# One transfer per store for the last two token tiles, a last half tile in two pieces, and a new issue order

## The chip, the cores and the metric

The kernel runs on one core of a Trainium2 chip. The metric is the device time of one execution in microseconds (us). The kernel before took 256.01 us as the median of three runs (255.62 to 257.51). One further execution was profiled; it took 256.55 us. A core has five engines that run their own instruction streams and meet at semaphores: PE (matrix multiply), DVE (vector), ACT (scalar functions, also copies), POOL, and SP, which here only issues DMA transfers. All numbers called "the profile" come from that one profiled execution, with times counted from the start of its span.

## The reference

For 2048 tokens of width 640, `x` is normalised (`xn`), and three things are added: `x` itself, a gated feed-forward block on `xn`, and a long convolution branch multiplied by `xn`.

```python
def _A_ref(q, k, v, shift_k, ssm_k, ssm_D):
    k_shift = sum(k_pad[:, t:t + S, :] * shift_k[:, ks - 1 - t] for t in range(4))
    kv = k_shift * v
    y = irfft2(rfft2(kv_pad) * rfft2(kf_pad))[..., :S, :]     # causal convolution of length 2048
    y = y + kv * ssm_D
    return q * y
def _B_ref(x, w_gate, w_up, w_down):
    return (sigmoid(x @ w_gate) * (x @ w_up)) @ w_down        # 640 -> 1728 -> 640
xn = layernorm(A_q)
out = A_q + _A_ref(xn, A_k, A_v, ...) + _B_ref(xn, ...)
```

Inputs and output are bfloat16, 2048 x 640.

## The kernel before, in words

**Token tiles.** The 2048 tokens are 16 tiles of 128 rows (`NQ = 16`). The tile `acc` [128, 16, 640] holds `x` at first and collects the result. Partition 32q + n of tile m holds token row 64n + 16q + m, so the output in memory, seen from a tile, has two outer dimensions: q (4 groups) and n (32 rows in each), the view `oq4` with axes q, n, m, d.

**Feed-forward block.** Four "rows" of four tiles (tr = 0 to 3). `rec_fc` (matmuls on line 770) computes a gate group and an up group for each of 14 blocks of 128 hidden columns, five matmuls of 512 columns each. ACT applies the sigmoid, DVE multiplies, and the product is written to `hT`. `rec_down` (line 786) multiplies `hT` by the down weights `wd`: for each token tile two halves of 320 output columns, each in two parts of seven matmuls. DVE adds each half from PSUM into `acc` (line 798). All these groups share two PSUM banks, named g: a new group waits until the group two places before it was read out. Weights for the gate and up groups come through four buffers named w.

**Convolution branch.** It is a four-stage transform over 10 sub-blocks of channels (two halves of five). Stage 1 is line 508, stage 2 line 528, the products lines 548 to 567, stage 3 line 580, stage 4 line 612. For sub-blocks 3 to 9 the products need the two partition halves exchanged, which two DMAs do (line 548, `P<-S`, the swap); the exchanged copy has one buffer. Stage 4 runs once per half, in four pieces (u = 0 to 3) of 128 small matmuls each; its result is multiplied and added into `acc` by DVE (lines 620 and 621). The tiles 14 and 15 of the down projection start only when all of that has been added (`PRM["ML"] = 14`).

**Stores.** `store` (line 630) writes ranges of tiles to `out`, in four DMAs of 32 partitions each (one per q), all issued by SP. The calls at the end of the kernel are for tiles 0-7, 8-11, 12-13, 14, the first half of tile 15 and the second half of tile 15.

**What sets the order.** Every operation is recorded by `plan.op` and gets a number. Nothing is scheduled at run time: the list `ORDER` names all numbers in the order in which they are emitted, and `ON_DVE` says which of the movable copies run on DVE instead of ACT. Each engine then executes its own operations in that order, waiting at each for its inputs and buffers. The numbers that the text below speaks of are these (they name the same operation in both lists):

- 80, 92: reciprocal and normalisation of token tile 1; 82, 83: statistics of token tile 2 (all DVE). 98: transposition of normalised tile 1 on PE.
- 653 and 654: transposition for the second row on PE, and the copy of its result out of PSUM.
- 872: gate group of hidden block 1, row 3. 887: the load of up weights for hidden blocks 4 to 7 of row 3; it reuses a w buffer. 893: the up group of block 5, row 3, the first user of that load in the new order.
- 549 to 555: stage 2 of the last sub-block. 557 and 558: its swap. 559 to 566: its products (DVE). 567 and 569: its stage 3 (PE). 911: the DVE product for hidden block 8 of row 3.
- 948 to 951: down projection of tile 14; 952, 953: its two additions. From 954 on the numbers differ between the lists: tile 15.

A few lines carry most of the ordering around the end:

```python
def table(self):
    dve = set(ON_DVE)
    for i in ORDER:
        o = self.ops[i]
        o.on = next(iter(o.engs)) if len(o.engs) == 1 else "DVE" if i in dve else "ACT"
    return [self.ops[i] for i in ORDER]
```

Of the kernel before, what the change touches and what calls it, by code (L numbers as in the profile page):

```python
# [16 lines left out]
ALU = mybir.AluOpType  # L17
# [4 lines left out]
P = 128  # L22
NQ = S // P
# [19 lines left out]
def _dft_tables():  # L43
# [34 lines left out]


ORDER = [  # L80
    3, 5, 0, 8, 2, 7, 6, 42, 71, 12, 10, 13, 4, 11, 72, 14, 16, 1, 19, 73, 74, 75, 91, 76, 607, 86, 608, 18, 43, 96,
    77, 61, 97, 78, 79, 104, 62, 63, 64, 81, 20, 80, 92, 87, 17, 82, 98, 83, 643, 15, 88, 84, 85, 148, 99, 93, 89,
    645, 100, 149, 60, 625, 644, 58, 90, 94, 67, 626, 102, 101, 27, 150, 103, 613, 621, 66, 44, 615, 623, 65, 106, 68,
    154, 622, 57, 624, 614, 616, 617, 619, 105, 153, 609, 56, 59, 22, 611, 618, 108, 620, 599, 601, 610, 612, 600, 29,
    107, 109, 646, 602, 157, 32, 158, 648, 603, 605, 112, 647, 650, 113, 30, 151, 649, 651, 652, 635, 637, 111, 110,
    152, 604, 636, 31, 606, 638, 23, 155, 26, 631, 627, 633, 632, 25, 156, 24, 629, 118, 117, 634, 21, 639, 641, 120,
    628, 630, 640, 642, 667, 35, 114, 661, 116, 668, 671, 115, 662, 665, 121, 119, 36, 133, 122, 123, 127, 681, 124,
    673, 39, 37, 682, 128, 684, 674, 677, 134, 45, 129, 679, 135, 653, 680, 38, 654, 683, 663, 131, 657, 136, 658,
    664, 33, 47, 666, 125, 48, 675, 126, 137, 34, 54, 172, 655, 656, 676, 163, 678, 669, 164, 659, 162, 130, 660, 28,
    670, 165, 672, 689, 691, 167, 739, 741, 132, 166, 181, 690, 692, 168, 53, 740, 721, 182, 742, 831, 723, 743, 693,  # L90
    744, 159, 298, 160, 41, 171, 722, 745, 724, 698, 40, 161, 700, 730, 169, 49, 732, 699, 701, 702, 52, 183, 832,
    734, 731, 300, 50, 178, 51, 736, 170, 173, 733, 175, 179, 735, 180, 174, 685, 176, 737, 738, 138, 177, 195, 687,
    196, 725, 727, 299, 199, 305, 186, 185, 184, 201, 202, 197, 46, 686, 688, 187, 188, 198, 189, 200, 203, 301, 833,
    707, 709, 190, 791, 69, 192, 302, 55, 726, 712, 194, 728, 193, 708, 729, 141, 70, 710, 213, 227, 191, 714, 214,
    713, 711, 139, 303, 228, 715, 215, 95, 716, 703, 718, 229, 304, 218, 217, 233, 230, 204, 206, 231, 704, 140, 142,
    216, 219, 771, 705, 706, 220, 234, 221, 208, 694, 696, 224, 695, 232, 697, 205, 717, 226, 249, 254, 719, 753, 225,
    207, 143, 222, 746, 772, 755, 720, 250, 209, 251, 754, 210, 253, 223, 757, 756, 252, 211, 758, 767, 759, 260, 235,
    237, 239, 212, 255, 263, 760, 256, 768, 236, 238, 261, 262, 288, 264, 290, 763, 265, 266, 267, 269, 770, 270, 241,
    242, 257, 240, 243, 244, 258, 834, 268, 836, 747, 285, 407, 748, 146, 289, 306, 751, 245, 271, 273, 412, 275, 291,
    286, 786, 247, 788, 749, 259, 287, 761, 318, 272, 294, 145, 762, 246, 750, 319, 297, 248, 752, 320, 321, 764, 324,  # L100
    325, 410, 274, 322, 276, 279, 409, 765, 280, 292, 787, 323, 277, 278, 766, 315, 789, 769, 835, 293, 326, 838, 308,
    309, 837, 327, 295, 296, 317, 281, 307, 839, 840, 310, 777, 282, 790, 779, 811, 283, 316, 778, 312, 782, 284, 328,
    329, 340, 354, 330, 331, 784, 783, 780, 334, 785, 341, 144, 773, 332, 342, 812, 360, 358, 355, 333, 413, 356, 774,
    311, 792, 781, 359, 345, 775, 361, 776, 357, 336, 813, 313, 335, 822, 338, 362, 815, 824, 408, 337, 823, 314, 339,
    363, 825, 376, 793, 795, 344, 351, 353, 343, 346, 794, 411, 147, 796, 817, 404, 347, 352, 427, 814, 819, 365, 364,
    366, 826, 428, 406, 429, 431, 367, 418, 816, 370, 405, 433, 371, 432, 828, 867, 368, 414, 383, 818, 374, 434, 369,
    797, 820, 821, 375, 799, 372, 373, 827, 348, 349, 829, 350, 798, 830, 384, 385, 430, 417, 435, 800, 387, 416, 419,
    415, 806, 436, 866, 424, 801, 386, 425, 808, 802, 377, 426, 421, 378, 379, 380, 388, 389, 803, 449, 390, 804, 463,
    450, 420, 805, 464, 422, 807, 437, 453, 860, 809, 451, 381, 841, 810, 465, 467, 468, 423, 382, 469, 470, 439, 854,
    397, 861, 864, 438, 391, 392, 855, 440, 858, 872, 394, 452, 441, 466, 455, 874, 848, 456, 460, 454, 849, 852, 393,  # L110
    462, 443, 856, 442, 398, 399, 857, 461, 400, 444, 445, 859, 401, 471, 844, 457, 447, 458, 459, 472, 446, 448, 490,
    473, 842, 485, 486, 499, 500, 845, 847, 474, 843, 846, 487, 501, 503, 504, 476, 475, 477, 479, 505, 478, 850, 506,
    489, 862, 496, 502, 498, 480, 863, 851, 481, 865, 482, 507, 873, 508, 483, 886, 887, 488, 853, 491, 493, 877, 497,
    492, 494, 527, 875, 878, 876, 510, 512, 515, 484, 529, 528, 531, 533, 879, 880, 516, 509, 532, 881, 534, 511, 513,
    514, 883, 868, 519, 530, 870, 395, 882, 520, 926, 884, 535, 536, 571, 869, 521, 523, 927, 871, 901, 495, 903, 885,
    892, 537, 396, 928, 402, 522, 585, 894, 902, 906, 524, 904, 526, 592, 539, 578, 893, 525, 538, 517, 888, 549, 541,
    895, 896, 518, 905, 550, 890, 897, 551, 907, 555, 553, 899, 540, 898, 543, 544, 542, 900, 929, 556, 545, 554, 552,
    931, 930, 557, 558, 889, 932, 908, 403, 891, 559, 910, 547, 909, 911, 921, 561, 563, 912, 923, 922, 560, 914, 924,
    548, 913, 917, 546, 915, 564, 567, 562, 565, 566, 569, 933, 568, 570, 579, 580, 916, 925, 934, 919, 581, 582, 918,
    935, 583, 920, 572, 936, 584, 573, 574, 937, 940, 575, 586, 576, 577, 962, 587, 938, 589, 588, 590, 960, 942, 939,  # L120
    591, 967, 966, 593, 594, 941, 595, 963, 596, 944, 597, 598, 943, 945, 946, 947, 968, 948, 950, 971, 969, 949, 964,
    961, 952, 951, 965, 953, 975, 970, 972, 974, 973, 954, 955, 958, 979, 976, 956, 978, 977, 9, 957, 959, 980, 982,
    981, 983
]
ON_DVE = [
    101, 103, 133, 34, 140, 144, 820, 568, 582, 574, 589, 588, 595
]


# [90 lines left out]
def kernel(  # L220
# [82 lines left out]
    def pe(dur, n, fn, **kw):  # L303
        plan.op({"PE": (dur * 1e-3, fn)}, ni=2 * n, **kw)
# [320 lines left out]

    def store(m0, m1, pri, d0=0, d1=DM):
        key = [("acc", m, x) for m in range(m0, m1) for x in range(4)] if d1 - d0 == DM else (
            [("fin", m, d0 // 320) for m in range(m0, m1)] + [("cv", m // 4) for m in range(m0, m1)])
        for q in range(4):
            dma(lambda e, q=q: e.dma_start(oq4[q][:, m0:m1, d0:d1], acc[32 * q:32 * q + 32, m0:m1, d0:d1]), 32,  # L630
                2 * (d1 - d0) * (m1 - m0), r=key, w=[("out", m0, d0, q)], pri=pri)
# [145 lines left out]
    def rec_down(tr, out):  # L777
        for t4 in range(4):
            m = 4 * tr + t4
            pd = [f"pd{m}_{i}" for i in range(2)]  # L780
            parts = [(0, 7, (0,)), (7, 14, (0,)), (0, 7, (1,)), (7, 14, (1,))]
            for c0, c1, ii in parts:
                def f(c0=c0, c1=c1, t4=t4, pd=pd, ii=ii):
                    for fc in range(c0, c1):
                        for i in ii:
                            nc.tensor.matmul(tl[pd[i]][:, 0:320], lhsT=hT[:, fc, t4 * P:(t4 + 1) * P],  # L786
                                             rhs=wd[:, fc, 320 * i:320 * i + 320],
                                             start=(fc == 0), stop=(fc == NFC - 1))
                kw = dict(r=[("hT", fc) for fc in range(c0, c1)] + [("wd", fc) for fc in range(c0, c1)] +
                          ([("z",)] if c1 == 14 else []) + ([("cv", u) for u in range(4)] if m >= PRM["ML"] and c0 == 0 else []) + ([("last",)] if m == NQ - 1 and c0 == 0 else []),  # L790
                          w=[(pd[i],) for i in ii] + ([("last",)] if m == NQ - 2 and c1 == 14 else []), pri=gt())
                if c0 == 0:
                    kw["alloc"] = [(pd[i], "g") for i in ii]
                n = len(ii) * (c1 - c0)
                pe(n * MD, len(ii) * (c1 - c0), f, **kw)
                pos[0] += n * MD * 1e-3
            for i in range(2):
                dve(320, 1, lambda i=i, m=m, pd=pd: nc.vector.tensor_tensor(  # L798
                    acc[:, m, 320 * i:320 * i + 320], tl[pd[i]][:, 0:320], acc[:, m, 320 * i:320 * i + 320], ALU.add),
                    r=[(pd[i],)], w=[("fin", m, i)], c=[("acc", m, q) for q in range(4)], pri=gt() - 2000)  # L800


# [90 lines left out]
    store(12, 14, 244.0)  # L893
    store(14, 15, 246.0)
    store(15, 16, 247.0, d1=320)
    store(15, 16, 248.0, d0=320)
    plan.emit(plan.table(), make)


# [28 lines left out]
```

## Time and profile before

| What | Value |
|---|---|
| Median of three runs | 256.01 us |
| Profiled execution, its own time | 256.55 us |
| Its span (first to last instruction) | 254.8 us (254.75) |
| PE busy / share of span | 241.0 us / 95% |
| DVE busy | 199.8 us / 78% |
| ACT busy | 179.0 us / 70% |
| Granted PE clock, mean | 0.998 |
| Stores to out: number, us from issue to landing | 24; 1.4 shortest, 2.3 median, 3.7 longest |

The profiled execution took 1.8 us more than its span; that part lies outside the recorded instructions. It is 0.54 us slower than the median of the three runs, so a difference worked out in the span is applied to the median. Rows of the profile name a line of the kernel, an engine, and the operation with the names of what it writes and reads. A bracket behind a row of the timeline says how long the engine had been idle before it and what ended that. "SPq" is SP's queue of issued DMAs; the time of such a row is the issuing, not the transfer. PE's busy time is an upper bound: matmuls overlap, so a row of 0.30 us can follow another after 0.136 us.

### The profile page before, as it was taken

The numbers are of one execution on the slowest core, as the hardware profiler recorded it, in microseconds if no ns is written. First come the engines' busy times: TensorE is split into PE (matmuls) and PEld (weight loads), VectorE is DVE, ScalarE is ACT, GpSimd is POOL, SyncE is SP. The second block draws the span as 40 slices with busy tenths as digits, with TensorE's granted clock in tenths as the row PEclk, the third lists the DMA queues.
The fourth block names the chain that finished last, engine by engine and source line by source line (L and its number), as shares of the span: only waits on it lengthen the run. The fifth ranks groups of instructions, "written<-read, shape, count | busy, mean of one in ns | idle before, by whom it ended". The sixth has DMA issues, their size and how long they took to land.

```text
span 254.8 us, 9455 instructions
## 1 busy us (share of the span) xinstructions
PE 241.0 (95%) x4231; PEld 145.1 (57%) x4231; DVE 199.8 (78%) x334; ACT 179.0 (70%) x263; POOL 0.7 (0%) x6
## 2 busy tenths in 40 slices
PE   7899999999999999999999999979999999898991
PEld 3654446664454657666564654656766465356770
DVE  5723347279999999999999999997999896878920
ACT  2737789975899986987798888846878895461300
POOL 1000000000000000000000000000000000000000
PEclk9999999999999999999999999999999999999999
DMA  6999999999989087698999757842127697000861
GB/s 179 335 250 317 246 256 135 143 184 192 153 196 290 5 227 187 95 144 118 166 226 234 194 163 190 100 111 59 35 55 233 148 300 214 3 3 23 191 156 53
DMA packets 91024, 41.44 MB, mean 163 GB/s; under 512 B 66656, under 2 KB 88104, under 8 KB 90664
## 3 DMA queue, kind: packets, MB, share of 16 engines
q1 hardware_dynamic: 90792, 40.52, 71.7%
q8 instruction: 33, 0.54, 0.9%
q10 hardware_dynamic: 192, 0.33, 0.4%
q14 instruction: 7, 0.06, 0.1%
HBM read 30.61 MB, written 5.24 MB: 141 GB/s over the span
## 4 chain that ended last, share of the span: by engine, by line
PE 59%; DVE 19%; ACT 9%; DMA 5%; issue 4%; ACTq 1%; SPq 0%; DVEq 0%
PE g L770 30%; PE g L786 16%; PE c L528 5%; DMA P<-S 3%; ACT jk L646 3%; PE c L612 3%; DVE kvt L488 2%; PE c L580 2%; DVE P L558 2%; ACT S L314 2%; DVE ta L475 2%; PE c L508 2%; DMA acc<-in_A_q_dram 2%; DVE tb L470 1%; PE c L750 1%
## 5 line engine op out<-in xcount | busy, mean ns | idle before, releaser
L770 PE MATMUL g<-xnT,w 128*128 128x512 bf16 x380 | 90.0, 379 | 0.9 <-DVE hT L737 0.7
L786 PE MATMUL g<-wd,hT 128*128 128x320 bf16 x448 | 66.6, 299 | 1.5 <-issue 0.8
L770 PEld LDWEIGHTS <-w 128*128 128x128 bf16 x380 | 35.0, 98 | 38.4 <-issue 1.2
L786 PEld LDWEIGHTS <-hT 128*128 128x128 bf16 x448 | 42.2, 98 | 19.0 <-issue 2.2
L314 ACT CAST S<-c 128x1024 bf16<-128x1024 f32 x40 | 39.7, 1027 | 3.9 <-PE c L528 3.8
L737 DVE TENSOR_TENSOR hT<-sig,g 128x512 bf16<-128x512 bf16 x32 | 21.9, 685 | 19.3 <-PE g L770 17.7
L770 PE MATMUL g<-xnT,V 128*128 128x512 bf16 x140 | 32.7, 379 | 0.0
L735 ACT ACTIVATE sig<-g 128x512 bf16<-128x512 f32 x32 | 19.3, 605 | 15.9 <-PE g L770 14.7
L798 DVE TENSOR_TENSOR acc<-g,acc 128x320 bf16<-128x320 f32 x32 | 15.5, 489 | 15.1 <-PE g L786 14.8
L528 PEld LDWEIGHTS <-Mt 64*128 64x128 f16 x1280 | 19.8, 95 | 5.4 <-issue 5.1
L314 ACT CAST T<-c 128x1024 bf16<-128x1024 f32 x20 | 19.8, 1020 | 3.6 <-PE c L508 3.5
L528 PE MATMUL c<-T,Mt 64*128 64x64 bf16 x1280 | 22.1, 190 | 0.0
L314 ACT CAST V<-c 128x1024 bf16<-128x1024 f32 x19 | 19.2, 1025 | 3.4 <-PE c L580 2.4
L488 DVE TENSOR_TENSOR kvt<-ta,vt 128x1024 bf16<-128x1024 bf16 x10 | 21.5, 2148 | 0.1
L770 PEld LDWEIGHTS <-V 128*128 128x128 bf16 x140 | 13.1, 98 | 14.7 <-issue 0.2
L317 ACT ACTIVATE T<-c 128x1024 bf16<-128x1024 f32 x20 | 20.3, 1039 | 0.8 <-PE c L508 0.8
L729 ACT ACTIVATE sig<-g 128x512 bf16<-128x512 f32 x18 | 10.9, 605 | 7.8 <-PE g L770 3.1
L475 DVE TENSOR_TENSOR ta<-ta,tb 128x1024 bf16<-128x1024 bf16 x20 | 13.8, 690 | 0.4
L470 DVE TENSOR_TENSOR tb<-kt,sT 128x1024 bf16<-128x1024 bf16 x20 | 13.7, 686 | 0.2
L561 DVE TENSOR_TENSOR S<-S 128x1024 bf16<-128x1024 bf16 x20 | 13.5, 687 | 0.3
L580 PEld LDWEIGHTS <-S 128*128 128x128 bf16 x160 | 10.9, 98 | 3.9 <-DVE S L567 1.2
L580 PE MATMUL c<-At,S 128*128 128x128 f16 x160 | 13.0, 219 | 0.0
(83 smaller groups left out, 241.2 us busy)
## 6 DMA issues: line engine op xcount, KB each, us to landing
w<-in_B_w_gate_dram SPq DMA_DIRECT2D x7, 640.0 KB, 5.7
w<-in_B_w_up_dram SPq DMA_DIRECT2D x7, 640.0 KB, 4.6
P<-S SPq DMA_DIRECT2D x14, 256.0 KB, 3.9
kt<-in_A_k_dram SPq DMA_DIRECT2D x8, 320.0 KB, 6.6
vt<-in_A_v_dram SPq DMA_DIRECT2D x8, 320.0 KB, 5.5
xnd<-xq SPq DMA_DIRECT2D x4, 640.0 KB, 4.7
ht<-in_A_ssm_k_dram SPq DMA_DIRECT2D x16, 96.0 KB, 4.3
wd<-in_B_w_down_dram SPq DMA_DIRECT2D x3, 480.0 KB, 8.6
```

What stands on the lines that cost most here:

```text
L314: fa = lambda: nc.scalar.copy(out=out_fn(), in_=in_fn())
L317: fa = lambda: nc.scalar.activation(out_fn(), in_fn(), ACT.Copy, scale=scale)
L470: dve(1024, 2, lambda: nc.vector.tensor_tensor(tl[c][:], sl(tl[kb], 3 - m), sh(m), ALU.mult) if c != o else nc.vector.tensor_tensor(tl[c]. ...
L475: dve(1024, 2, lambda: nc.vector.tensor_tensor(tl[a][:], tl[a][:], tl[c][:] if c != o else tl[c].rearrange("p b n j -> p n b j"), ALU.add) ...
L488: dve(1024, 1 if kt else 2, lambda: nc.vector.tensor_tensor(by_j(tl[o]) if kt else tl[o][:], tl[a].rearrange(form), sl(tl[vb], 0).rearrang ...
L528: nc.tensor.matmul(tl[c][:, b, 64 * kk:64 * kk + 64], lhsT=Mb[rows, k, 64 - 64 * r:192 - 64 * r], rhs=tl[T][rows, 2 * k + r].rearrange("p ...
L580: nc.tensor.matmul(o, lhsT=tl[S_][:, b, 0, j, :], rhs=Ab[:, 2 if zc else 0, :], start=True, stop=zc)
L735: act(512, lambda: nc.scalar.activation(tl[sg][:], pv(0), ACT.Sigmoid), r=[pk(0)], w=[(sg,)], alloc=[(sg, "sig")], pri=pri - 2000)
L737: dve(512, 1, lambda: nc.vector.tensor_tensor(hT[:, fc, :], tl[sg][:], pv(1), ALU.mult), r=[pk(1), (sg,)], w=[(hk, fc)], pri=pri - 2000)
L770: nc.tensor.matmul(tl[c][:], lhsT=w()[:, k, o:o + P], rhs=tl[X][:, k, :], start=(k == 0), stop=(k == NC - 1))
L786: nc.tensor.matmul(tl[pd[i]][:, 0:320], lhsT=hT[:, fc, t4 * P:(t4 + 1) * P], rhs=wd[:, fc, 320 * i:320 * i + 320], start=(fc == 0), stop=( ...
L798: dve(320, 1, lambda i=i, m=m, pd=pd: nc.vector.tensor_tensor(acc[:, m, 320 * i:320 * i + 320], tl[pd[i]][:, 0:320], acc[:, m, 320 * i:320 ...
```

## The change

Four things change. `store` issues one DMA over all 128 partitions when its first tile is 14 or 15, with q and n as the two outer dimensions on the memory side; the stores of tiles 0 to 13 stay four DMAs each. The second half of tile 15 is split into columns 320-479 and 480-639, each with its own PSUM bank, its own 14 matmuls of 160 columns, its own addition and its own store. The stores go from 24 DMAs to 16. `ORDER` and `ON_DVE` are replaced by new lists; the movable copies on DVE go from 13 to 17.

```diff
 ORDER = [
-    3, 5, 0, 8, 2, 7, 6, 42, 71, 12, 10, 13, 4, 11, 72, 14, 16, 1, 19, 73, 74, 75, 91, 76, 607, 86, 608, 18, 43, 96,
...
-    961, 952, 951, 965, 953, 975, 970, 972, 974, 973, 954, 955, 958, 979, 976, 956, 978, 977, 9, 957, 959, 980, 982,
-    981, 983
+    1, 42, 5, 0, 6, 8, 7, 71, 72, 10, 12, 13, 11, 14, 73, 74, 75, 91, 86, 16, 87, 607, 76, 608, 4, 96, 77, 78, 97, 79,
...
+    966, 968, 952, 951, 969, 958, 953, 975, 954, 959, 962, 978, 955, 971, 960, 976, 956, 957, 961, 977
 ]
 ON_DVE = [
-    101, 103, 133, 34, 140, 144, 820, 568, 582, 574, 589, 588, 595
+    101, 103, 45, 133, 654, 136, 134, 34, 139, 426, 525, 895, 915, 575, 582, 589, 595
 ]
@@ store
-            [("fin", m, d0 // 320) for m in range(m0, m1)] + [("cv", m // 4) for m in range(m0, m1)])
+            [("fin", m, (d0 > 0) + (d0 > 320)) for m in range(m0, m1)] + [("cv", m // 4) for m in range(m0, m1)])
+        if m0 >= PRM["ML"]:
+            dma(lambda e: e.dma_start(oq4[:, :, m0:m1, d0:d1], acc[:, m0:m1, d0:d1]), 128,
+                2 * (d1 - d0) * (m1 - m0), r=key, w=[("out", m0, d0)], pri=pri)
+            return
@@ rec_down
+            cols = [(0, 320), (320, 480), (480, 640)] if m == NQ - 1 else [(0, 320), (320, 640)]
+            pd = [f"pd{m}_{i}" for i in range(len(cols))]
+            for i, (d0, d1) in enumerate(cols):
+                for c0, c1 in ((0, 7), (7, 14)):
+                    def f(c0=c0, c1=c1, t4=t4, pd=pd, i=i, d0=d0, d1=d1):
+                        for fc in range(c0, c1):
+                            nc.tensor.matmul(tl[pd[i]][:, 0:d1 - d0], lhsT=hT[:, fc, t4 * P:(t4 + 1) * P],
+                                             rhs=wd[:, fc, d0:d1], start=(fc == 0), stop=(fc == NFC - 1))
...
@@ calls
-    store(15, 16, 248.0, d0=320)
+    store(15, 16, 248.0, d0=320, d1=480)
+    store(15, 16, 249.0, d0=480)
```

At the end of the two lists, read per engine, stand these operations. Before: PE computes tile 14 (first half, second half, in interleaved parts), tile 15's first half, its second half; SP issues four stores for tile 14, four for the first half of tile 15 and four for its second half, last. New: after tile 14 PE computes part one of columns 480-639, part one of columns 0-319, part two of 480-639, part two of 0-319, then columns 320-479 whole; SP issues the store of tile 14, of columns 480-639, one of the four stores of tiles 12-13, the store of columns 0-319, and last that of columns 320-479.

In the first microseconds DVE's list changes from "statistics of tile 1, half the statistics of tile 2, 80, 92, rest of tile 2" to "statistics of tile 1, statistics of tile 2, 80, 92", and ACT computes the mean of tile 3 one place earlier. The copy 654 moves from ACT to DVE. Between 872 and 893 PE now has three other feed-forward groups, three stage-2 groups and one stage-1 group. Between the last stage-2 group of the last sub-block and its first stage-3 group PE had eleven feed-forward groups and two stage-3 groups; it now has nine and two. DVE now runs 911 before 559, and products 559, 560, 561, 562, 565, 566 before 569.

## The prediction

> **What bounds the kernel now.** I read the windows by stage first, then the timeline of the end, then PE's waits. The columns of the windows are PE, PEld (weight loads), DVE and ACT busy us with instruction counts, POOL, granted clock, DMA share, GB/s.
>
> ```profile
> 180.00:200.00 20.00, 20.00 (x409) 12.81 (x402) 19.27 (x32) 16.66 (x21) 0.00 (x0) 1.00 0.39 108
> 200.00:220.00 20.00, 19.15 (x254) 10.17 (x253) 15.39 (x23) 13.25 (x18) 0.00 (x0) 1.00 0.74 197
> 235.00:249.00 14.00, 13.94 (x221) 9.87 (x218) 7.99 (x13) 2.18 (x3) 0.00 (x0) 1.00 0.75 173
> 249.00:255.00 6.00, 0.04 (x1) 0.00 (x0) 0.49 (x1) 0.00 (x0) 0.00 (x0) 0.90 0.15 39
> ```
>
> PE is full until 249.0 at full clock. Then it is done, and almost 6 us pass with one DVE instruction and a little DMA traffic. So the time is PE's stream, with few holes, plus a tail. From 60 to 200 DVE is 96% busy as well (133.9 of 140 us in the windows), so an order has little room on either engine there. The tail:
>
> ```profile
> 248.74 0.30 PE L786 MATMUL g<-wd,hT 128*128 128x320 bf16 x1
> 249.01 3.62 SPq L630 DMA_DIRECT2D out_dram<-acc  x8
> 249.08 0.49 DVE L798 TENSOR_TENSOR acc<-g,acc 128x320 bf16<-128x320 f32 x1 [1.41 <-PE g L786]
> ```
>
> The last matmul ends at 249.04, the last addition at 249.57. But SP is still issuing the four stores of the first half of tile 15 (one each 0.46 us), so the first store of the second half goes out only at 250.87 and the fourth at 252.20. It lands at 253.72, 1.52 us after its issue began: 0.92 to its first data packet, 0.23 of data, 0.37 until SP sees the semaphore. Then come 1.03 us of final semaphore work to 254.75:
>
> ```profile
> L923 SPq EVENT_SEMAPHORE  x7: 17/28/28, 253.3 to 254.7; - x7
> ```
>
> From the last matmul's end to the span's end: 5.71 us. PE's waits before that:
>
> ```profile
> PE c L612 <- issue: 2.1, 4, 0.7
> PE g L786 <- issue: 0.8, 1, 0.8
> PE g L770 <- DVE hT L737: 0.7, 1, 0.7
> PE g L705 <- DVE xq L683: 0.7, 1, 0.7
> PE g L786 <- ACT xnT L314: 0.4, 1, 0.4
> ```
>
> Holes over 0.05 us between matmuls add to 6.2 us. That is all that any order can gain on PE; there is no such limit on what it can lose.
>
> **Tail, first part: PE's last tile.** Before, tile 15 is 28 matmuls of 320 columns, one each 0.136 us. New, 14 of those stay and 28 of 160 columns come. Their spacing is not in the trace; the bounds are 0.056 (128 columns, line 580) and 0.098 (one weight load, if it is no longer hidden). Halving 0.136 gives 0.069, which I take, as weight loads of 0.098 hide at 0.056 already. So 28 x 0.069 - 14 x 0.136 = +0.03 us (-0.3 to +0.8). A wait is added: there are two g banks, and the third group after tile 14 needs the bank of tile 14's second half, read out by the addition that ends at 245.77 in the old order; PE gets there after 7 x 0.069 us from 245.07, at 245.56, and starts at 245.82 (a PE start follows such an addition by 0.05). That is +0.26; behind it stands only PE's own stream. Last matmul's end: 249.33, with its shorter drain.
>
> **Tail, second part: stores.** The last addition has 160 columns. From the rows of 512 columns (685 ns) and 320 (489) one column costs 1.02 ns, so it takes 0.33: 249.37 to 249.70. The addition of columns 0-319 ends at 248.90, its store is issued at 248.93 and occupies SP for 0.42 to 0.73 us (the shortest usual issue, and the one of `ssm_D`, line 395, the only row with outer dimension 4). Either way SP is free at 249.73, and the queue that cost 1.3 us is gone. Data begin 0.92 later, at 250.65. How many DMA engines carry it decides the rest. A 32-partition store closes with 16 completion packets, two data packets per engine. The `ssm_D` load closes with 4, so I take 4 engines for an outer dimension of 4: 32 packets each. A 640-byte packet takes 32 ns and a 160-byte one 14 ns; for 320 bytes I take 20 (bounds 14 and the 55 of a 1280-byte packet). The store of columns 0-319 holds the same 4 engines for 32 x 32 ns from 249.85, to 250.87. So the last data end at 250.87 + 0.64 = 251.51, and with 0.37 + 1.03 the span ends at 252.9: **-1.85 us**, PE's +0.29 included. With 16 engines it is 252.2 (-2.55); with 55 ns packets 254.0 (-0.7).
>
> The Trainium skill, page "DMA: Bandwidth & Descriptors", section "Why a DMA increments its semaphore by 16 and not by 1", gives the rule behind the 4: the engines used are the largest number up to 16 that divides the slowest dimensions of both sides, here 128 and 4. By it the tail gains 1.85, without it 2.55. Its section "Specifications" speaks against the change: below 512 bytes a transfer does a read-modify-write. No row here shows a write to memory that short (the least is 640 bytes).
>
> **The order, start.** Tile 1's normalisation (80, 92) moves behind the rest of tile 2's statistics (82 second half, 83).
>
> ```profile
> 7.97 0.45 DVE L683 TENSOR_SCALAR xq<-acc,st 128x640 bf16<-128x640 bf16 x1
> 8.47 0.45 PE L705 MATMUL g<-ident,xq 128*128 128x128 bf16 x5 [0.71 <-DVE xq L683]
> ```
>
> PE waits for exactly this. The inserted 0.48 + 0.21 delay 98 to 9.16. Behind it the 20 matmuls of line 750 no longer wait for tile 2 (0.24 in the old order), so the net is +0.45 (0 to +0.7).
>
> **The order, second row.** 0.39 us were lost at 49.3 for a copy on ACT. Copy 654 moves to DVE (0.49 against 0.67) and PE has two more groups ahead: -0.3 (-0.4 to +0.5).
>
> **Weight load 887.** It reuses the buffer that 872 reads last, and 893 needs it. Between them PE has 3 x 1.08 + 3 x 0.51 + 0.37 = 5.14 us. Two loads of this size issued with little else in flight landed after 4.48 and 4.55 us; the same load among others took 8.3 (190.06 to 198.35). The swap of sub-block 8 is issued right behind it. I take 5.2 plus 0.25 for the semaphore: +0.3 (0 to +3.4).
>
> **Last sub-block.**
>
> ```profile
> 217.65 0.69 DVE L552 TENSOR_TENSOR P<-S,P 128x1024 bf16<-128x1024 bf16 x1 [1.99 <-DMA P<-S]
> 218.99 4.48 PE L770 MATMUL g<-xnT,w 128*128 128x512 bf16 x20 [0.69 <-DVE hT L737]
> ```
>
> DVE sat 1.99 us before the swapped data, and 911 behind it held PE for 0.69. In the new list 911 stands ahead of 559, so that wait goes. What is late next: stage 2 to stage 3 had 12.8 us of PE work between them and has 10.6 now. The chain between is 2.4 (copies), 5.3 (swap), 6 products x 0.70: 11.9. So PE waits about 1.25 instead of 0.85 (0.69 and 0.16): +0.4 (-0.85 to +2.2, when all eight products are needed as before).
>
> **Bursts of small matmuls.** The waits called "issue" (2.93 us in five holes from 156 to 233) follow runs of line 612. In the old order the densest 7 us of PE work hold 806 PE instructions, in the new 696; the densest 11 us hold 1104 in both. I take -0.4 (-2.9 to +1).
>
> ACT loses 3.2 us of work and DVE gains 2.9, nearly all outside 60 to 200; both have cover there, 12.6 of 15 us busy at most: 0.
>
> **Sum:** -1.85 + 0.45 - 0.3 + 0.3 + 0.4 - 0.4 = -1.4. Span 253.35, own time 255.15. The profiled execution (256.55) lies 0.54 above the median of 256.01, so the forecast is **254.6 us**.
>
> **Rivals.** (1) *The order closes holes.* Two burst holes and both other waits go (-1.7) and 16 engines carry the stores (-2.55), with the start's +0.45: -3.8, 252.2. For it: the bursts are spread in the middle. Against: the densest 11 us are not. (2) *The weight load is late*, so slower: 887 lands after 8.3 us as it did before, PE stands 3.4 us at 893 instead of 0.3, +1.7 in all: 257.7. It decides against the change from a landing of 6.6 us. For it: two 320 KB loads go out just ahead on SP, the swap just behind. Against: those loads should have moved by then. (3) *The tail gives little*: 55 ns per short packet, gain 0.7 instead of 1.85: 255.75. No row prices such a packet, so it has a small chance. By the short-write rule of the Trainium skill quoted above this would be the way.
>
> **Chances.** Forecast 0.5, rival 1 0.2, rival 2 0.2, rival 3 0.1. The range runs from rival 1 to rival 2: 252.2 to 257.7; the forecast's own is 253.2 to 255.8. About 1% (2.56 us) is what a measurement of this kernel tells from no change: faster than 253.45 takes most of rival 1 and a little of the forecast, 0.24; slower than 258.57 takes the far end of rival 2 and unseen waits of an order changed in some 280 PE groups, 0.12; 0.64 stays within.
>
> **What would show it.** Last matmul near 249.3 plus what the order costs; last addition 0.33 us; SP idle before the last store; 5.71 us from PE's end to the span's end becoming about 3.6; 4 completion packets per joined store; PE's wait at 8.5 growing by 0.7; a wait of PE on a weight load near line 770 around 200 (rival 2) or on line 567 before line 580 near 222. The prediction is wrong if holes appear between 60 and 200, where I count nothing.

## The result, and the profile after

The changed kernel takes 254.6 us (median of 13 runs, 253.29 to 255.3) against 257.4 us for the kernel before in runs beside it (13 runs, 255.62 to 258.81). The ratio is 0.990, with a 95% interval of 0.988 to 0.993. The profiled execution took 254.63 us; its span is 252.8 us (252.76), 1.99 less than before.

The number forecast was 254.6. The way to it was another one, and luck had a part in the number: it stands on a kernel before of 256.01 us, which took 257.4 in the runs beside this one. Here are the windows of the end and the timeline of SP and DVE there; the columns of the windows are PE, weight loads, DVE and ACT busy us, POOL, granted clock, DMA share, GB/s.

```profile
235.00:249.00 14.00, 11.91 (x191) 8.94 (x190) 6.50 (x12) 0.69 (x1) 0.00 (x0) 1.00 0.60 146
249.00:251.00 2.00, 0.00 (x0) 0.00 (x0) 0.00 (x0) 0.00 (x0) 0.00 (x0) 1.00 0.25 67
249.00:253.00 4.00, 0.00 (x0) 0.00 (x0) 0.00 (x0) 0.00 (x0) 0.00 (x0) 0.79 0.12 34
```

```profile
244.62 1.93 SPq L629 DMA_DIRECT2D out_dram<-acc  x2
245.63 0.32 DVE L800 TENSOR_TENSOR acc<-g,acc 128x160 bf16<-128x160 f32 x1 [1.69 <-PE g L789]
...
246.61 0.48 SPq L633 DMA_DIRECT2D out_dram<-acc  x1
247.19 1.25 SPq L629 DMA_DIRECT2D out_dram<-acc  x2
247.55 0.33 DVE L800 TENSOR_TENSOR acc<-g,acc 128x160 bf16<-128x160 f32 x1 [0.48 <-PE g L789]
```

PE is done at 247.51, 1.53 us earlier than before (249.04); the prediction had it 0.74 later. The last addition ends at 247.88 and SP is idle before the last store, as forecast: it is issued at 247.90. But from PE's last matmul to the end of the span 5.25 us pass, where before it was 5.71 and the prediction said 3.6. The last store's first data packet starts at 249.93, 2.03 us after the issue (0.92 was assumed), its last at 251.05; SP sees it at 251.75, and the final semaphore work takes 1.0.

PE's waits in the changed kernel:

```profile
PE c L818 <- DVE sig L807: 1.6, 1, 1.6
PE c L611 <- issue: 1.3, 2, 0.8
PE c L579 <- DVE S L566: 0.7, 2, 0.5
PE g L708 <- DVE xq L686: 0.6, 1, 0.6
```

The holes called "issue" are fewer than before (2.93 us with those at line 786), but two are left, at 230.87 and 234.64.

To see where PE gained, I summed over PE's list, in its order, the least time of each kind of matmul (0.216 us for 512 columns, 0.136 for 320, 0.056 for 128, and so on down) and subtracted that sum from the time at which PE got there. What remains is the time lost so far. It goes by weight loads: the page of the changed kernel has 4245 of them and only 4211 matmuls, so 34 matmul records are missing and small holes between matmuls in it mean nothing. The values are good to about 0.3 us (0.7 at 220), since at one time the two lists are at different work. Lost time after, less that before:

| at us | 10 | 30 | 50 | 60 | 160 | 180 | 200 | 220 | 230 | 240 | last load |
|---|---|---|---|---|---|---|---|---|---|---|---|
| difference | +0.1 | 0.0 | -0.5 | -0.4 | +0.3 | -2.2 | -1.7 | -1.8 | -2.8 | -1.8 | -1.4 |

One stretch, 160 to 180, gives 2.1 to 2.5 us. Everything else together costs about 1. In before, in and around this stretch, stand these rows (PE's timeline; x is the number of matmuls in a row of one kind, the bracket the idle time before it):

```profile
155.57 0.86 PE L612 MATMUL c<-V,Bt 32*32 32x80 bf16 x84
157.00 0.52 PE L612 MATMUL c<-V,Bt 32*32 32x80 bf16 x44 [0.56 <-issue]
...
165.20 0.27 PE L612 MATMUL c<-V,Bt 32*32 32x80 bf16 x20
166.21 1.06 PE L612 MATMUL c<-V,Bt 32*32 32x80 bf16 x108 [0.74 <-issue]
...
171.21 0.41 PE L508 MATMUL c<-Ft,kvt 32*128 32x64 f16 x32 [0.86 <-ACT xq L314]
```

A stage-4 piece is 128 matmuls that depend on nothing new between the 84th and the 85th, and yet PE stops there. The holes at 166, 171 and 175 (0.74, 0.86 and 0.53) add to 2.13 us, nearly all that the stretch gives. In the changed kernel the same pieces run through between 160 and 176, and two later ones are cut:

```profile
164.94 0.69 PE L611 MATMUL c<-V,Bt 32*32 32x80 bf16 x64
165.56 0.64 PE L527 MATMUL c<-T,Mt 64*128 64x64 bf16 x32
166.13 0.69 PE L611 MATMUL c<-V,Bt 32*32 32x80 bf16 x64
...
230.36 0.51 PE L611 MATMUL c<-V,Bt 32*32 32x80 bf16 x42
231.40 0.28 PE L611 MATMUL c<-V,Bt 32*32 32x80 bf16 x22 [0.53 <-issue]
...
234.35 0.29 PE L611 MATMUL c<-V,Bt 32*32 32x80 bf16 x28
235.40 0.99 PE L611 MATMUL c<-V,Bt 32*32 32x80 bf16 x100 [0.76 <-issue]
```

Counting every weight load, matmul and semaphore instruction of PE in the trace as one, the first weight load behind each of these holes has something in common with the others:

| kernel | PE goes on at (us) | its instruction number | modulo 256 |
|---|---|---|---|
| before | 157.00, 166.21, 171.21, 174.94, 229.85 | 4546, 5057, 5314, 5570, 7617 | 194, 193, 194, 194, 193 |
| after | 231.40, 235.40 | 7874, 8130 | 194, 194 |

The page counts the transfers that bring instructions:

```profile
q8 instruction: 33, 0.54, 1.0%
```

33 transfers of 16 KB for 8,500 PE instructions is one per 256. Each of the holes above ends 1.25 to 1.52 us after such a transfer ended (155.49 to 157.00, 164.92 to 166.21, 230.15 to 231.40). So the theory that the experiments had to test is **F**: PE stands when it reaches the end of a block of 256 instructions before the next block has come. (The other letters, A, B and C, are given anew in each expectation.) The Trainium skill, page "Runtime: NRT & Kernel Launch", section "Instruction fetch mechanics", says that engines refill their instruction memory in 16 KiB blocks of 256 instructions through a DMA queue of their own, and that the cost of a block boundary is mostly hidden. The size agrees with this trace; the cost does not, with 0.5 to 0.9 us per hole in these two traces.

### The profile page after: what moved, and what is told of

The parts are those of the page before. It is cut to its first block, busy times and chain, and to the rows that moved or that the text cites. A ratio compares the mean times of both kernels' runs of the same rounds, so it can differ in the third digit from the quotient of the medians.

```text
span 252.8 us, 9452 instructions
## 1 busy us (share of the span) xinstructions
PE 239.6 (95%) x4211; PEld 145.6 (58%) x4245; DVE 202.2 (80%) x339; ACT 177.2 (70%) x260; POOL 0.7 (0%) x6
## 4 chain that ended last, share of the span: by engine, by line
PE 66%; DVE 14%; DMA 7%; ACT 5%; issue 3%; ACTq 1%; SPq 0%; DVEq 0%
PE g L773 29%; PE g L789 20%; PE c L527 5%; PE c L611 3%; DMA P<-S 3%; PE c L579 3%; DMA w<-in_B_w_up_dram 2%; PE c L507 2%; ACT S L313 2%; DVE ta L474 2%; PE c L753 2%; DMA acc<-in_A_q_dram 1%; ACT sig L738 1%; DVE kvt L487 1%; DVE hT L740 1%
## 5 line engine op out<-in xcount | busy, mean ns | idle before, releaser
L773 PE MATMUL g<-xnT,w 128*128 128x512 bf16 x355 | 89.1, 379 | 2.4 <-DVE hT L740 0.5
L789 PE MATMUL g<-wd,hT 128*128 128x320 bf16 (+1 forms) x462 | 66.3, 295 | 0.2
L789 PEld LDWEIGHTS <-hT 128*128 128x128 bf16 x462 | 42.9, 98 | 16.8 <-issue 0.7
L313 ACT CAST V<-c 128x1024 bf16<-128x1024 f32 x20 | 20.4, 1026 | 4.8 <-PE c L579 3.7
L800 DVE TENSOR_TENSOR acc<-g,acc 128x320 bf16<-128x320 f32 (+1 forms) x33 | 15.6, 477 | 9.6 <-PE g L789 9.3
L313 ACT CAST T<-c 128x1024 bf16<-128x1024 f32 x18 | 17.9, 1021 | 1.7 <-PE c L507 1.7
```

What stands on the lines that cost most here:

```text
L313: fa = lambda: nc.scalar.copy(out=out_fn(), in_=in_fn())
L773: nc.tensor.matmul(tl[c][:], lhsT=w()[:, k, o:o + P], rhs=tl[X][:, k, :], start=(k == 0), stop=(k == NC - 1))
L789: nc.tensor.matmul(tl[pd[i]][:, 0:d1 - d0], lhsT=hT[:, fc, t4 * P:(t4 + 1) * P], rhs=wd[:, fc, d0:d1], start=(fc == 0), stop=(fc == NFC - 1))
L800: dve(d1 - d0, 1, lambda i=i, m=m, pd=pd, d0=d0, d1=d1: nc.vector.tensor_tensor(acc[:, m, d0:d1], tl[pd[i]][:, 0:d1 - d0], acc[:, m, d0:d1 ...
```

## The experiments

All ratios are to the kernel before, from runs on the same chip, with 95% intervals.

**Order alone, end alone.** The first takes the new `ORDER` and `ON_DVE` on the old code; the second the old list on the new code, with the new end behind it.

```diff
 # order alone: code of before, lists of after; where the new list has a joined store:
-    975            # tile 14, one transfer
+    975, 972, 974, 973   # tile 14, one per q; tile 15 likewise, its second half in one piece
 # end alone: code of after, list of before up to 951, then
+    958, 953, ..., 975, 954, 959, 962, 978, 955, 960, 976, 956, 957, 961, 977
```

> The new issue order with the old end: tile 14 and both halves of tile 15 stored 32 partitions at a time, the last half tile in one piece. Theory A (the gain is PE's stream; the joined stores give little): PE's last matmul ends 1.5 us earlier than before, as it does with the whole change, and then 5.7 us pass as before, so the span is about 253.2 and the ratio to before 0.994. Theory B (the prediction's sum: the order costs 0.45 us, the end gives 1.85): span about 255.2, ratio 1.002. The two differ in where the last matmul ends: 247.5 (A) or 249.5 (B).

> The old issue order up to the second tile of the last four, then the new end: joined stores from tile 14 on, the last half tile in two pieces. Theory A: the last matmul ends at 249.1 to 249.4, then 5.25 us as in the changed kernel: span about 254.5, 0.2 us less than before, ratio 0.999. Theory B (the prediction's sum of the end): the last matmul ends at 249.3 and 3.6 us follow: span 252.9, ratio 0.993.

Order alone: 0.990 (0.986 to 0.993), as much as the whole change. In its trace the last matmul ends at 246.22 and the span is 251.6. End alone: 0.998 (0.995 to 1.001); last matmul 249.30, span 254.5, 5.2 us behind PE. Theory A (PE's stream is the gain) holds in both in direction: the order is the gain, and the joined stores with the split give at most half a per cent, if anything. Its size was missed in the first: PE was done 1.3 us earlier than the 247.5 of A, in a profiled execution (253.38) that is the fastest of six. The split and the joining were not tried apart. The trace of end alone also carries a warning. It has the old list, and its holes in the stretch from 155 to 177 are 0.56, 0.19 and 0.53 us, where before lost 0.56, 0.74, 0.86 and 0.53. How much a boundary costs differs between traces of one list, so what the order gained at which place is not settled by two traces; that it gained is, by the medians. In order alone SP was never idle behind 242.50:

```profile
242.50 6.97 SPq L631 DMA_DIRECT2D out_dram<-acc  x14
```

The span ends 5.4 us behind PE's last matmul, against 5.25 in the changed kernel.

**What is long in the new end.** One more store joined, for tiles 12 and 13.

```diff
-        if m0 >= PRM["ML"]:
+        if m0 >= PRM["MJ"]:        # MJ = 12
```

> The changed kernel, with the stores of tiles 12 and 13 joined into one transfer as well (one issue in place of four). Theory A (all joined stores go through the same 4 DMA engines, one behind the other): it puts 64 more packets of 71 ns, 4.5 us, on those 4 engines just ahead of tile 14's 2.3 us, so the data of the last store end about 2 to 2.5 us later than in the changed kernel (251.07 there): span about 255, ratio 1.000 to 1.003 to before, although PE does nothing else. Rival C (a joined store simply has a longer way from issue to data, 1.5 to 2 us, whatever is in front of it): three issues fewer on SP, the last store starts no later, span 252.5 to 252.8, ratio 0.990.

1.004 (1.002 to 1.007), 1.4% slower than the changed kernel with three DMA issues fewer. PE's last matmul ends at 247.78, but the last store's data end at 254.38 in place of 251.07: 3.3 us later, more than the 2 to 2.5 expected. About 1.2 us of it is on SP: one single issue lasted 2.60 us, the store of tile 14 was issued at 246.29 in place of 244.62, and the last store at 249.12 in place of 247.90. The rest lies behind that issue: 3.39 us to the first data in place of 2.03, and 1.87 us of data in place of 1.14. Rows of the DMA view from 240 on (KB of each, median us from issue to landing) for the stores of 160 KB of the earlier tiles, first after, then this run:

```profile
out_dram<-acc SPq DMA_DIRECT2D x4, 160.0 KB, 3.1
```

```profile
out_dram<-acc SPq DMA_DIRECT2D x4, 160.0 KB, 6.9
```

So rival C of this run falls and its theory A stands: joined stores share four engines. The trace of the changed kernel shows the row of them. Each joined store closes with 4 completion packets (seen best in the run with early stores, below, where the four stores lie apart). Tile 14's 128 packets of 1280 bytes (71 ns each) run from 246.15 to 248.87, the next store's from 248.24, the next from 248.97, the last from 249.93 to 251.07. On four engines that is 32 x (71 + 20 + 36 + 20) = 4.7 us of packets in 4.9 us: they are busy from tile 14 to the end. The window from 249 to 251 above says the same: a DMA share of 0.25 is 4 of the 16 engines, and from 249.93 to 250.51 packets of the last two stores alternate on them. The Trainium skill, page "DMA: Bandwidth & Descriptors", section "Why a DMA increments its semaphore by 16 and not by 1", says besides the number that it is the lowest-numbered engines that such a transfer uses; that would put all four stores on the same ones, as this row shows.

**Two queues.** The joined stores undone, half of the transfers from ACT; and later, on top of the early stores of the next experiment, only the last piece that way.

```diff
 # tiles 14 and 15 (first run), or only columns 320-479 of tile 15 (second run)
+        dma(..., 32, ..., q="ACT" if q > 1 else "SP", ...)
```

> The changed kernel with its joined stores undone: tile 14 and the three pieces of tile 15 go out 32 partitions at a time, two of the four transfers of each from SP's queue and two from ACT's, which has nothing else to do then. Theory A (what is long in the new end is the 4 engines): each transfer is spread over 16 engines again, SP issues 2 x 0.46 us per piece, the last one of SP starts at about 248.8 and lands 1.5 us later, then 1.03 us: span about 251.3, ratio 0.985. Rival C (the length lies in how late the last addition ends and in the way from issue to data of any store at this point, 2 us with the others in flight): span about 252.5, ratio 0.989. If two queues disturb each other, no gain: 252.8 or more.

> The kernel with the early stores (the run before this one with that change) and one more edit: the last piece of 160 columns goes out 32 partitions at a time, two transfers from SP's queue and two from ACT's, which is idle then. Theory A (the last joined store waits behind the joined store of columns 0 to 319 on the same 4 DMA engines: 1.39 us from its issue to its first data): four transfers over 16 engines, the last issue 0.4 us after the last addition, landing 1.5 us later: about 0.5 less than with early stores alone, span 250.5, ratio to before 0.986. Rival: two queues disturb each other, or ACT waits for a semaphore as SP did in the earlier run with two queues: 251 or more.

0.999 (0.997 to 1.001) and 1.005 (1.003 to 1.007): both misses, on the side of the rival. In the second run SP's stores for tile 14 and on stood still, though tile 14 was added up at 243.27:

```profile
239.84 1.25 SPq L635 DMA_DIRECT2D out_dram<-acc  x3
248.69 1.95 SPq L631 DMA_DIRECT2D out_dram<-acc  x3
250.74 0.91 SPq L635 DMA_DIRECT2D out_dram<-acc  x2
```

```profile
SPq L631 <- DMA out_dram<-acc: 7.5, 1, 7.5
```

SP waits for a DMA there: for semaphore 104, which ACT's store of the last piece, issued at 247.23, had taken. In the first run SP's store at 246.39 waits likewise for semaphore 108 of an ACT store issued at 245.00. Here the two queues draw on the same DMA semaphores, and a store that stands earlier in `ORDER` can be made to wait for a later one. The transfers themselves were quick: ACT's store issued at 245.00 had its data out by 246.0. How the semaphores are dealt out was not tried.

**Early stores.** SP's list only: the stores of tiles 0 to 7 and 8 to 11 directly behind the additions that complete them, and the four of tiles 12 and 13 together behind theirs. In the changed kernel one of those four stands between the joined stores, at 246.61. First with the joined stores, then with order alone's old end.

```diff
-    963, 965, ..., 970, 964, ..., 973, 974, 967, ..., 972, ..., 966, ..., 968, ..., 969, ..., 971
+    584, 577, 963, 965, 964, 966, ..., 591, 967, 968, 969, 970, ..., 946, 971, 972, 973, 974
```

> The changed kernel with one thing moved on SP's queue: the remaining stores of tiles 0 to 7 go right behind the first two of them (232 in place of 240 to 244), those of tiles 8 to 11 behind the third convolution addition (236). PE's order is untouched. If SP's queue or the 16-engine stores that it sends late hold up the joined stores (theory A's second half), tile 14's store is issued at 244.0 in place of 244.62, the piece of 320 columns finds no other traffic, and the span falls by 0.6 to 1.2 to about 251.8. If only the row of joined stores on their own 4 engines counts (4.7 us of packets from tile 14's first), the gain is the earlier start alone, 0.6 or less.

> The new issue order with the old end (32 partitions at a time, the last half tile in one piece) and the early stores of tiles 0 to 11: the counterpart of the run with early stores, without its joined transfers. SP has then only tile 14 (4 x 0.46) and the two halves of tile 15 (8 x 0.46) to issue after 243.5. Theory A (joining saves issues on SP, 2 us, and pays for it with the row on 4 engines): the last issue starts at 248.6 to 249.0, lands 1.5 later, span 251.1 to 251.6, about the same as with the joined stores (251.0): ratio 0.989 to 0.991. If joining is what makes the end short once SP is free, it is 252.0 or more, 0.993. If joining only costs, 250.5 or less, 0.986.

0.988 (0.985 to 0.991; span 251.0) and 0.988 (0.984 to 0.992; span 250.9). With SP free, tile 14's joined store goes out when its addition ends (243.51), in the second run the four single ones from 243.31 on; that one row covers all 18 issues up to the end:

```profile
243.51 4.47 SPq L631 DMA_DIRECT2D out_dram<-acc  x4
```

```profile
237.37 11.45 SPq L631 DMA_DIRECT2D out_dram<-acc  x18
```

Last data end at 249.53 and 249.56. The first run's span was forecast at 251.8 or later, so both branches of that expectation were too small; 0.46 of its gain of 1.7 is an earlier end of PE (247.05). Joined or not is the same again. With joined stores the last issue comes 0.39 us behind PE's end, with single ones 1.84: 1.45 saved. From that issue to the last data it is 2.09 against 1.16: 0.93 paid on the four engines. The split last tile costs PE 0.30 us more, and 0.1 to 0.2 is left of it. These are the fastest kernels of the study, but the intervals do not tell them from the changed kernel's (0.988 to 0.993).

**Theory F: move the block boundaries, and nothing else.** In the warm-up, whose result nobody reads, 4 matmuls of 512 columns become 36 of 64. That is 64 PE instructions more, ahead of everything, in time that PE waits out.

```diff
-        for _ in range(n):                       # n = 12: matmuls of 512 columns
+        for _ in range(8 if n == 12 else n):
             nc.tensor.matmul(tl["wps"][:, 0], lhsT=tl["warm"][:, 0:P], rhs=tl["warm"][:], start=True, stop=True)
+        for _ in range(36 if n == 12 else 0):
+            nc.tensor.matmul(tl["wps"][:, 0, 0:64], lhsT=tl["warm"][:, 0:P], rhs=tl["warm"][:, 0:64], start=True, stop=True)
```

> The changed kernel with 32 more tiny matmuls in the warm-up (36 of 64 columns in place of 4 of 512), where PE waits for its first input anyway: 64 PE instructions more, nothing else. Theory F (PE stands because the next 256 instructions, one 16 KB fetch, have not come; each fetch costs at least about 3.7 us from block to block): the stalls again come at instruction 193 or 194 modulo 256, which is now 64 instructions earlier in the work. In the trace of the changed kernel the blocks cut that way would take 2.7 us at 159.5, 1.5 at 166.5, 3.1, 3.1, 2.8 and 1.7 at 227 to 235, so new holes of 1 to 2 us come near 159 and 166, those at 230.9 and 234.6 leave their matmuls for others, and the span grows by 2.5 to 5: 255.3 to 257.8. Rival W (the stalls belong to the work, for instance to waits of the stage-4 bursts on PSUM copies): the holes stay at the same matmuls of line 611, the span at 252.8.

1.020 (1.014 to 1.026), span 258.0: 3% slower than the changed kernel with 32 tiny matmuls more at the start. PE's timeline:

```profile
158.67 0.53 PE L611 MATMUL c<-V,Bt 32*32 32x80 bf16 x45
159.90 0.27 PE L611 MATMUL c<-V,Bt 32*32 32x80 bf16 x19 [0.70 <-issue]
...
166.36 0.57 PE L611 MATMUL c<-V,Bt 32*32 32x80 bf16 x50
168.65 0.25 PE L611 MATMUL c<-V,Bt 32*32 32x80 bf16 x14 [1.72 <-issue]
...
235.65 0.58 PE L789 MATMUL g<-wd,hT 128*128 128x320 bf16 x3
236.89 0.70 PE L789 MATMUL g<-wd,hT 128*128 128x320 bf16 x4 [0.66 <-issue]
237.52 1.19 PE L611 MATMUL c<-V,Bt 32*32 32x80 bf16 x124
241.17 0.21 PE L611 MATMUL c<-V,Bt 32*32 32x80 bf16 x4 [2.45 <-issue]
```

The pieces that ran through at 159.15 and 166.13 in the changed kernel are cut now. The pair that was cut there after 28 of its 128 matmuls (234.6) is cut after 124, and even a group of seven long matmuls of line 789 is cut after three. The four holes are at instructions 4802, 5314, 8130 and 8386: all 194 modulo 256, as is a fifth of 0.38 us at 186.38 (6082). The places expected near 159 and 166 are there, and the growth of 5.2 is just above the 2.5 to 5 expected. Rival W (the stalls belong to the work) falls.

Not all of the 3% is holes. Right behind the two longest ones the granted clock (the column before the DMA share) is 0.50:

```profile
170.00:173.40 3.40, 3.40 (x44) 1.83 (x43) 3.33 (x5) 3.37 (x5) 0.00 (x0) 0.50 0.02 8
241.70:245.00 3.30, 3.30 (x15) 1.83 (x13) 1.68 (x3) 0.42 (x1) 0.00 (x0) 0.50 0.03 5
```

There matmuls of 320 columns follow each other every 0.267 us in place of 0.136, so each of the two stretches costs about 1.7 us. No other trace of this case has such a stretch before PE's end. Whether the holes brought it on is open: a hole of 2.63 us in a later run was not followed by one.

Where PE was stopped at a boundary in this run, it crossed 3.43 to 4.28 us after the one before.

**Theory F: spread the dense work.** Same instructions, other order of PE's groups from 224 on, DVE's additions moved along; a strong version, the strong version with the early stores, a mild version, and the mild one with early stores and the two-queue end.

```diff
 # PE's groups: 572 ... 594 are stage 4, 933 a gate group, 936-945 down projections of tiles 12, 13, 948 tile 14
-    572, 573, 933, 938, 579, 580, 944, 945, 586, 939, 587, 936, 593, 594, 942, 937, 943, 948
+    572, 573, 933, 938, 944, 579, 939, 580, 945, 936, 586, 942, 587, 937, 943, 593, 594, 948   # strong
+    572, 573, 933, 938, 579, 580, 944, 945, 939, 586, 936, 587, 942, 593, 594, 937, 943, 948   # mild
```

> The changed kernel with the same instructions in another order from 224 on: the down-projection groups of tiles 12 and 13 stand between the eight stage-4 bursts (9 long groups between the first and the last burst in place of 6). Theory F: no 256 instructions take less than 3.7 us any more, so the holes at 227.6, 230.9 and 234.6 (0.3 + 0.5 + 0.8) go and the last matmul ends at 245.3 to 246 in place of 247.5. The span gains less, since the last stores wait for SP and the four DMA engines: about 252.2 in place of 252.8. Rival W: the bursts stand for their copies, the holes remain or grow, last matmul at 247.5.

> Both at once: long groups between the bursts and the early stores early. Theory F and A together: last matmul at 245.5, tile 14's joined store issued at about 242.5, its 4 engines busy till about 246.5, the last joined store issued at 246.0 and its data done by 249.9: span 251.3, ratio about 0.983 to before. If the two do not add up, 252.

> The changed kernel with PE's groups from 226 to 239 in another order, milder than the first such run: only two groups move ahead of the last bursts, so that each 256 PE instructions from 224 to 240 hold 3.3 to 4.1 us of work (3.2, 3.2, 3.3, 4.7 in the changed kernel; 4.7, 4.0, 4.2, then 3.2 in the first such run, where the stall moved to the fourth block). Theory F: stalls of 0.45 us in place of 1.5, last matmul at 246.5; the stores behind it keep the span at about 252.4, ratio 0.989. Rival W: the order of the groups does not matter for the stalls, 252.8 and 247.5.

> Early stores, the last piece over two queues, and the milder spread together. If they add up: last matmul at 245.8 to 246.3, span 249.8 to 250.2, ratio 0.983. If the early stores' data lie in front of the instruction fetches between 232 and 240 (the fetch of block 31 started 3.1 us after the block in the run with early stores, 1.1 in the changed kernel), the spread gives a stall of 1 to 2 us at instruction 8386 and the span is 251 to 252.

The ratios: 0.999 (0.997 to 1.001), 1.000 (0.997 to 1.003), 0.993 (0.990 to 0.995) and 1.006 (1.003 to 1.009). No version gained; the expected times were all missed. The traces tell why. In the strong version the three holes from 227 to 235 are gone, with blocks of 4.7, 4.0 and 4.2 us, but the next block of 256 holds only 2.3 us of work, and PE stops at its end, at instruction 8386, 194 modulo 256:

```profile
236.98 1.23 PE L613 MATMUL c<-V,Bt 32*32 32x80 bf16 x128
238.14 1.12 PE L791 MATMUL g<-wd,hT 128*128 128x320 bf16 x7
240.17 2.06 PE L791 MATMUL g<-wd,hT 128*128 128x320 bf16 x14 [0.91 <-DVE vt L621]
```

With the early stores the same instruction waits three times as long:

```profile
237.52 1.12 PE L791 MATMUL g<-wd,hT 128*128 128x320 bf16 x7
241.28 1.93 PE L791 MATMUL g<-wd,hT 128*128 128x320 bf16 x13 [2.63 <-DVE acc L622]
```

The fetch for that block started 0.76 us after PE had crossed into the block before in the first of the two runs, and 2.45 us after it in the second, where the stores keep the DMA engines at a share of 0.97 from 236 to 238 (0.77 in the first). That fits stores whose data lie in the way of the instructions, as far as two single traces can show it. The second of them is the fastest of its ten executions (254.21, 2.0 us below their median), so it does not show what the others lost. The names in the brackets (two different DVE additions) are the last semaphore events before the hole, not its cause: the count modulo 256 and the fetch say what it is.

The mild version shows F's other side: the holes at 227 and 231 are gone, 0.17 is left at 235, and no block boundary stops PE for longer. But the group 948, now earlier, needs a g bank that DVE has not read out, since DVE is in the convolution's products:

```profile
239.25 0.97 PE L791 MATMUL g<-wd,hT 128*128 128x320 bf16 x6 [1.18 <-DVE acc L802]
```

This one is at 180 modulo 256 and is what it says. The last matmul ends at 247.31, 0.2 earlier than in the changed kernel, and in the strong version without early stores it is the same (247.28, with another new wait of 0.45 on DVE at 227.32). So PE gained less than the 1.0 to 2.2 us expected in these two, and the end behind it lost more than that: it is 6.13 us in the mild version and 7.10 in the strong one, where the changed kernel has 5.25, and tile 14's store is issued at 244.89 and 245.91 there, not at 244.62. In the strong version, SP's earlier stores wait for additions of the convolution that now come later. The fourth run has the same hole (1.45) and SP's wait for ACT's semaphore on top.

## Why the prediction was right in its number and wrong in its steps

- **Tail, PE's last tile.** The spacing of 0.069 us was right, also the last addition's 0.33. The wait for the third bank was 0.26 as forecast (0.331 us from one matmul to the next at 243.67, where 0.069 is usual), and from the end of tile 14's second addition PE needs 3.56 us where before it needed 3.27: the +0.29 came true.
- **Tail, stores: the first term that failed.** It was -1.85 with PE's +0.29 included; measured behind PE's last matmul, -0.46 in place of -2.1. The parts were right one by one: 4 engines (4 completion packets), 20 ns for a packet of 320 bytes, SP idle before the last store. Wrong was what lay on the four engines ahead of it: I counted the store of columns 0 to 319 alone. Tile 14's store, 2.3 us of packets, and that of columns 480 to 639 come before it on the same four, and the row does not run empty before the end. The step "data begin 0.92 later" (1.14 with the wait for the engines) was 2.03, the data took 1.14 and not 0.64, and SP saw the end after 0.68 and not 0.37; the final 1.0 was right. These add up to the 1.7. With the extra joined store it got 3.3 us worse.
- **Order, bursts: the other term that failed.** Forecast -0.4 (-2.9 to +1); -2.1 to -2.5 between 160 and 180, within the bounds and far from the value. I had seen that the holes follow runs of line 612 and that the density of instructions mattered, but compared the densest 7 and 11 us of the two lists. What counts is each block of 256 instructions, where its ends fall and when its fetch began. With that, the places of possible holes could have been named; their sizes differ between traces of one list.
- **Start.** Forecast +0.45; 98 started 0.25 us later than before (8.72, not 9.16), and from the 60th weight load on (10.7 us) nothing of it is left. PE's wait there did not grow by 0.7, it is 0.65 in place of 0.71: the data of tile 1 came earlier, and DVE began its statistics of that tile at 5.86, where before it was 6.16.
- **Second row.** Forecast -0.3; -0.7 between 40 and 50, the hole at 49.3 and some more.
- **Weight load 887.** Forecast +0.3 and rival 2 (3.4 us). PE shows no wait on a load near 200; rival 2 did not come.
- **Last sub-block.** Forecast +0.4; PE's wait for the products at 219.84 is 0.50 where before 0.69 and 0.16 were lost, -0.35.
- **60 to 160, counted at nothing:** 0.7 us more lost. The prediction had called itself wrong if holes appear between 60 and 200; the largest new one there is 0.47 us, at 133.1.

The two failed terms are of about the same size, 1.7 too much gain in the stores and about 2 too little in the bursts, and cancel; that is why the sum of -1.4 came out near the -1.99 measured in the spans. That is luck. So is the hit on 254.6 to the digit: in medians the gain was 2.8 us, from 257.4, not 1.4 from 256.01. Rival 1 named the right mechanism for the order (burst holes close) and the wrong one for the stores (16 engines). Rival 3's place was right, the tail gave little, but not by its price: a short packet costs 20 ns, not 55. The short-write rule of the Trainium skill (page "DMA: Bandwidth & Descriptors", section "Specifications") would make a 320-byte packet dear; at 20 ns beside 36 ns for 640 bytes, no run here shows such a price.

A caution on the small terms: seven traces with the same PE list before the last tile (after, order alone, the extra joined store, both two-queue runs, both runs with early stores) have their last matmul between 246.2 and 247.8. About 0.3 of this is the split of the last tile; the rest, some 1.3 us, is what two single traces can differ by without any change in that list. The sizes of the terms from "Start" on are not settled by them.

## What to carry to other kernels

Where PE issues hundreds of small matmuls, count its instructions in blocks of 256. The blocks that stopped PE at their end for more than 0.45 us here held 1.7 to 4.15 us of work, but a short block need not do it: one of 2.72 us, from 150.94 in the changed kernel, passed without a stop, since its fetch had begun at 150.50, before PE reached it. Any PE instruction added or removed earlier moves all the ends. The stores with 4 as the outer dimension on the memory side saved issues here but used four DMA engines, and several in a row waited for one another; price the whole row, not the last. Before merging transfers at the end, look whether the queue ahead of them could simply have been emptied sooner.

## What was not expected of the hardware

- A PE stall can be an instruction fetch: 0.5 to 2.6 us each, over nine of the traces 22 holes of more than 0.45 us, each at 193 or 194 modulo 256 and each ending 1.20 to 1.59 us after a 16 KB transfer. The profile calls them "issue", or names an engine that has nothing to do with them.
- 32 tiny matmuls at the start, in time that PE waits out, made the kernel 3% slower: by holes at other block ends, and by two stretches of 3.4 us at a granted clock of 0.50, whose cause is open.
- Fetches start 0.76 to 1.44 us after PE's first instruction of the block before them in a quiet stretch of the traces (222 to 234, DMA share 0 in between). With a DMA share above 0.85 the same step took 0.65 to 3.16 us: often no longer, at times much.
- DMAs issued from SP and from ACT share their semaphores, and SP stood 5.4 us for one of ACT's.
- The issue of a single store on SP took up to 2.60 us in the run with the extra joined store (0.42 usual).
